# Gates of two token blocks by seven quarter products instead of eight, in a fused retention and feed-forward kernel

## The chip, the core and the metric

The kernel runs on one core of a Trainium2 chip. Its engines work side by side, each on its own queue of instructions: PE multiplies matrices (PEld is its loading of weights, which overlaps), DVE, ACT and POOL do elementwise work, and SP issues transfers. PE puts its results in PSUM, which the kernel's pools divide into eight banks of 128 x 512 float32 (`tr` 1, `qk` 2, `pv` 1, `st` 1, `ffn` 3); the other engines read them from there. The metric is the time of one execution in microseconds on the device, the median of the runs.

## The reference

Retention for 8 sequences of 8 heads, and a gated feed-forward layer on its result:

```python
scores = scale * np.matmul(q, k.transpose(0, 1, 3, 2))       # q, k, v: 8 x 8 x 576 x 64
Dmat = np.where(rel >= 0, gamma[:, None, None] ** rel[None, :, :], 0.0)
attn = np.matmul(scores * Dmat[None, :, :, :], v)
x = attn.transpose(0, 2, 1, 3).reshape(4608, 512)
gate = 1.0 / (1.0 + np.exp(-(x @ w_gate)))                   # w_gate, w_val: 512 x 1536
val = x @ w_val
out = gate * val @ w_out                                     # w_out: 1536 x 512
```

## The kernel before, in words

Both halves are interleaved: while PE does the feed-forward products of one block of tokens, the retention of the tokens of the next one is put between them. The tokens come in blocks: 0 to 511 first (written out by hand), then two of 256 tokens at 512 and 768 (`BLOCKS`), then blocks of 512 from 1024 on. The retention makes x transposed in bfloat16 (`xT`, model dimension on the partitions), in pairs of steps: `row` (q times k), `pt` (times the decay, on DVE), `new` (the step's share of the running state), `s` (the state's sum, on DVE), `sb` (the state cast to bfloat16, on ACT) and `val` (the result, cast into `xT` by ACT). Before that, POOL and DVE scale q and k by the decay (`qk`), POOL casts v, and SP's transposing transfers (or PE's `turn`, copied out as `T`) turn them.

The 1536 columns of the feed-forward layer are 12 chunks of 128 (`fc`), four to a unit u. In a block of 512 tokens, a unit's gates, a product of 512 x 512 by 512 x 512, are formed from quarters by seven products (`quarter_units`): product 1 is x's first quarter by the weights' first quarter, 2 the second quarters, 3 the fourth x quarter with a sum of weights, 4 a sum of x quarters (`xsum`) with the fourth weight quarter, and 5, 6 and 7 sums of weights by sums of x. In code: product 1 goes to bank `a` (`gatea`) and ACT copies it to bank `g` (`gateg`), on which product 2 adds; product 6 adds to `a`, and ACT keeps a copy `u2`; product 5 goes to bank `e` (`gatee`), and ACT keeps a copy `s5`; product 3 adds to `e`, and DVE adds `e` to `u2`; product 7 adds to `a`, and DVE adds `a` to `s5`; product 4 adds to `a`. Each of the four results gets its sigmoid on ACT. A product is four matmuls, of 128 x 128 weights by the quarter's columns. The weight sums (`wgt_sb` for gates, `wvt` for values, `wt_sb` for the output weights) are made once by DVE or POOL, before the block that first needs them.

In the two blocks of 256 tokens, gates and values are formed by full products (`h_units`): 12 groups of eight matmuls of 256 columns for each block, a gate pair `h_g` and its value pair `h_v` by turns, a sigmoid on ACT for each gate pair, a multiply on DVE for each value pair. Then come two output products (`op_units`) of 12 matmuls of 512 columns, which ACT copies to `ob` to be stored.

The order on every engine is the order in which the code is written (`manual_schedule`). In the blocks of 256, `ffn_units` yields after each group, and behind the i-th group of block w the loop at the end of the kernel puts what the table `SUMS_AT` lists for "w.i": weight sums (g, w, o, with their number and engine, v for DVE and p for POOL), the scaling and casting of later steps (c), a turn (t), the first batch's state (f); `PAIRS_AT` says behind which groups a pair of retention steps begins. `OP_CUTS` and `FIRST_OP_CUTS` say how many matmuls of 512 columns of the output products are cut into two of 256.

Of the kernel before, what the change touches and what calls it, by code (L numbers as in the profile page):

```python
# [9 lines left out]
FP32 = mybir.dt.float32  # L10
# [6 lines left out]
def kernel(  # L17
# [858 lines left out]
    def h_units(gvs, fcs, t0, n):  # L876

        for fc in fcs[::2]:
            gv_tile(gvs, t0, fc)
            both = made[t0, fc // 4][:, fc % 4:fc % 4 + 2, 0:n]  # L880
            for what, w_sb in (("g", wg_sb), ("v", wv_sb)):
                ps = ffn_psum.tile([P, 2, n], FP32, tag="ffn", name=f"h_{what}_{t0}_{fc}")
                for i in range(2):
                    for kc in range(NKC):
                        nc.tensor.matmul(ps[:, i], lhsT=w_sb[:, kc, (fc + i) * P:(fc + i + 1) * P],  # L885
                                         rhs=xT(kc, slice(t0, t0 + n)), start=(kc == 0), stop=(kc == NKC - 1))
                if what == "g":
                    nc.scalar.activation(out=both, in_=ps, func=AF.Sigmoid)
                else:
                    nc.vector.tensor_tensor(out=both, in0=both, in1=ps, op=ALU.mult)  # L890
                yield 8 * n
# [79 lines left out]
    first_w = {}  # L971

    def first_sums_begin(kind):

        u = NU - 1
        t = [osb.tile([P, 2, 2, 2 * P], BF16, tag="osb", name=f"first_{kind}_{i}") for i in range(1 if kind == "g" else 2)]
        first_w[kind] = ([wt3_sb["g"][i][u] for i in range(3)] if kind == "g" else
                         [t[0][:, 0], t[0][:, 1], t[1][:, 1]]) + [t[-1][:, 0]]

    def first_w_sum(kind, i, eng):  # L980

        a11, a12, a21, a22 = w_quarters(kind, NU - 1)
        s1, s2, s4, s3 = first_w[kind]
        to, a, b, op = ((s1, a21, a22, ALU.add), (s2, s1, a11, ALU.subtract), (s3, a11, a21, ALU.subtract),
                        (s4, a12, s2, ALU.subtract))[i]
        eng.tensor_tensor(out=to, in0=a, in1=b, op=op)

    def first_x_sum(i, eng):

        if 0 not in turned_x:  # L990
            turned_x[0] = [ld_pool.tile([P, 2, 2, 256], BF16, tag="xsum", name=f"xsum_0_{i}", bufs=SLOTS["xsum"])
                           for i in range(2)]
        t1, t2, t3, t4 = (turned_x[0][i][:, j] for i in range(2) for j in range(2))
        b11, b12, b21, b22 = (xT(slice(r, r + 2), slice(c, c + 256)) for r in (0, 2) for c in (0, 256))
# [7 lines left out]
    def quarter_units(gvs, t0):  # L1002

        BANKS = {("g", 0): [(tr_psum, "tr"), (pv_psum, "pv"), (qk_psum, "qk")],
# [4 lines left out]
                 ("w", 2): [(qk_psum, "qk"), (qk_psum, "qk"), (tr_psum, "tr")]}  # L1009
        waiting = []  # L1010
# [5 lines left out]
        def bank(kind, u, i):  # L1016
            pool, tag = BANKS[kind, u][i]
            more = {"written": True} if pool is ffn_psum and i == 1 else {}
            name = ("gate" if kind == "g" else "w") + "age"[i]
            return pool.tile([P, 2, 256], FP32, tag=tag, name=f"{name}_{t0}_{u}", **more)  # L1020

        def keep(kind, u, name, ps, eng=on_act):
            t = sum_tile([P, 2, 256], FP32, f"{kind}{name}_{t0}_{u}")
# [3 lines left out]
        def right(i):  # L1027
            x = xT(ALL, slice(t0, t0 + 512))
            t = turned_x[t0] if i > 3 else None
# [661 lines left out]
```

## Time and profile before

| | us |
|---|---|
| median of 3 runs | 303.05 (302.89 to 303.10) |
| the profiled execution | 303.61 |
| its span | 302.0 |
| PE busy in the span | 295.4 |
| first group of block 512 starts | 51.52 |
| first output product of block 512 starts | 63.20 |
| first group of block 768 starts | 69.78 |
| first output product of block 768 starts | 81.70 |
| block 1024 starts | 88.62 |

The span runs from the first to the last record of the execution, so 1.6 us of it lie around it. Times of rows are counted from the span's start. A row of a timeline gives start, duration (of the whole run of like instructions, "x8"), engine, line of the kernel, operation, output and inputs with the program's names, and in brackets the idle time before it with what ended it. In a row of grouped instructions the busy time and the mean duration in ns stand behind the bar. Matmul durations overlap, and their distance is read from the starts.

### The profile page before, as it was taken

To read this page: it belongs to the slowest core of one execution; us is meant where nothing else is said; L and a number is where in the kernel's file an instruction comes from. 1 tells how busy PE (TensorE), PEld (TensorE's weight loads), DVE (VectorE), ACT (ScalarE), POOL (GpSimd) and SP (SyncE) were. 2 spreads that over 40 slices of the span, in tenths; PEclk is the share of its full clock that TensorE was granted. 3 is DMA by queue.
4 is the path that set the end of the run, shared out by engine and by line. 5 is a ranking of instruction groups with operands and counts; after the bars stand their busy time and mean duration, and the time that the engine had idled before them with its cause. 6 is when DMAs were issued, how large, how long until landed. Compare 5 with 4: busy or idle time off the path is not lost.

```text
span 302.0 us, 10689 instructions
## 1 busy us (share of the span) xinstructions
PE 295.4 (98%) x4430; PEld 250.4 (83%) x4437; DVE 230.1 (76%) x439; ACT 204.6 (68%) x414; POOL 224.9 (74%) x253
## 2 busy tenths in 40 slices
PE   8999999999999999999999999999999999999994
PEld 3687876978868888888888888888888888888883
DVE  5967995686886998789748974896489848935793
ACT  6764574345369747985798589857985698559830
POOL 5775754846479898978997898789978947860780
PEclk9999999999999999999999999999999999999999
DMA  7999999979899979897759967976793165004013
GB/s 205 309 339 398 362 345 239 209 155 210 174 197 222 248 176 225 186 221 211 143 114 200 250 143 155 194 207 146 128 204 127 37 111 205 4 2 139 3 36 104
DMA packets 146464, 54.99 MB, mean 182 GB/s; under 512 B 124400, under 2 KB 139760, under 8 KB 146416
## 3 DMA queue, kind: packets, MB, share of 16 engines
q1 hardware_dynamic: 145328, 53.59, 73.3%
q10 hardware_dynamic: 1088, 0.72, 0.8%
q8 instruction: 34, 0.56, 0.8%
q14 instruction: 14, 0.11, 0.1%
HBM read 37.75 MB, written 9.44 MB: 156 GB/s over the span
## 4 chain that ended last, share of the span: by engine, by line
PE 86%; DMA 7%; SPq 4%; POOL 1%; issue 0%; ACT 0%; DVE 0%
PE gatea L1045 12%; PE wa L1045 12%; PE qa L1172 11%; PE qe L1172 9%; PE gatee L1045 6%; PE we L1045 6%; PE h_v L885 4%; PE h_g L885 3%; PE op L1305 3%; DMA wv<-in_moe_w_val_dram 3%; PE op L1548 3%; PE gateg L1045 3%; PE wg L1045 3%; SPq L186 3%; DMA wg<-in_moe_w_gate_dram 2%; PE val L717 2%
## 5 line engine op out<-in xcount | busy, mean ns | idle before, releaser
L1045 PEld LDWEIGHTS <-wg_sb 128*128 128x128 bf16 x348 | 34.0, 98 | 4.2
L1072 POOL TENSOR_TENSOR gv<-gv,wu 128x512 bf16<-128x512 bf16 x20 | 23.5, 1174 | 16.1 <-DVE wu L1084 16.0
L1172 PEld LDWEIGHTS <-gsum 128*128 128x128 bf16 x312 | 29.9, 98 | 3.7
L1045 PEld LDWEIGHTS <-wv_sb 128*128 128x128 bf16 x296 | 29.0, 98 | 3.4
L429 POOL TENSOR_TENSOR qk<-q,qtab 128x512 bf16<-128x512 f32 x28 | 30.1, 1073 | 1.4 <-DMA q<-in_q_dram 1.4
L1084 DVE TENSOR_TENSOR gu<-gatee,gu 128x512 f32<-128x512 f32 x22 | 15.2, 690 | 19.4 <-ACT gateg L1076 10.2
L1045 PEld LDWEIGHTS <-wgt_sb 128*128 128x128 bf16 x264 | 25.8, 98 | 3.0
L942 POOL TENSOR_TENSOR gsum<-gsum,gv 128x256 bf16<-128x256 bf16 (+1 forms) x20 | 17.6, 891 | 14.4 <-DVE gsum L942 12.6
L1045 PE MATMUL gatea<-xsum,wg_sb 128*128 128x256 bf16 x172 | 25.6, 273 | 0.0
L1172 PEld LDWEIGHTS <-gv 128*128 128x128 bf16 x228 | 21.8, 98 | 2.7
L429 POOL TENSOR_TENSOR qk<-k,ktab 128x512 bf16<-128x512 f32 x11 | 12.1, 1097 | 13.9 <-DMA k<-in_k_dram 9.6
L1087 DVE TENSOR_TENSOR gs<-gatea,gs 128x512 f32<-128x512 f32 x22 | 15.1, 688 | 9.4 <-PE gatea L1045 9.3
L942 POOL TENSOR_TENSOR gsum<-gv,gsum 128x256 bf16<-128x256 bf16 (+1 forms) x24 | 21.9, 921 | 0.2
L703 DVE TENSOR_TENSOR pt<-row,tri 128x512 bf16<-128x512 f32 x30 | 19.2, 681 | 2.9 <-PE row L686 2.7
L442 POOL TENSOR_TENSOR v<-v,ktab 128x512 bf16<-128x512 f32 x19 | 20.9, 1100 | 0.0
L1045 PE MATMUL wa<-xsum,wv_sb 128*128 128x256 bf16 x136 | 20.4, 273 | 0.0
L658 ACT CAST sb<-s 128x512 bf16<-128x512 f32 (+1 forms) x26 | 14.3, 569 | 8.4 <-DVE s L828 8.3
L787 ACT CAST xT<-val 128x512 bf16<-128x512 f32 x26 | 14.7, 592 | 7.0 <-PE val L733 7.0
L942 DVE TENSOR_TENSOR gsum<-gv 128x512 bf16<-128x512 bf16 (+1 forms) x34 | 18.7, 576 | 0.0
L1045 PEld LDWEIGHTS <-wvt 128*128 128x128 bf16 x168 | 16.4, 98 | 1.9
L942 POOL TENSOR_TENSOR gsum<-gv 128x256 bf16<-128x256 bf16 (+1 forms) x20 | 17.6, 880 | 0.0
L1070 ACT ACTIVATE gv<-gu 128x512 bf16<-128x512 f32 x22 | 14.0, 638 | 5.2 <-DVE gu L1084 5.2
(210 smaller groups left out, 882.6 us busy)
## 6 DMA issues: line engine op xcount, KB each, us to landing
k<-in_k_dram SPq DMA_DIRECT2D x26, 256.0 KB, 3.8
q<-in_q_dram SPq DMA_DIRECT2D x26, 256.0 KB, 4.2
v<-in_v_dram SPq DMA_DIRECT2D x26, 256.0 KB, 4.6
out_dram<-ob SPq DMA_DIRECT2D x24, 256.0 KB, 2.8
wg<-in_moe_w_gate_dram SPq DMA_DIRECT2D x12, 256.0 KB, 5.3
wv<-in_moe_w_val_dram SPq DMA_DIRECT2D x12, 256.0 KB, 5.2
wo<-in_moe_w_out_dram SPq DMA_DIRECT2D x12, 256.0 KB, 5.3
v32p<-in_v_dram SPq DMA_DIRECT2D x6, 256.0 KB, 4.7
```

What stands on the lines that cost most here:

```text
L429: eng.tensor_tensor(out=to, in0=by_halves(loaded[s][1 - i]), in1=tab, op=ALU.mult)
L442: nc.gpsimd.tensor_tensor(out=natural["v", s], in0=loaded[s][2], in1=tab, op=ALU.mult)
L658: eng(out=both_steps["sb", b, c][:, js], in_=both_steps["s32", b, c][:, js])
L703: nc.vector.tensor_tensor(out=t[:, y, 0:n].rearrange("p i m t -> p (i m) t"), in0=rows_tile[ss[0]][y][:, 0:n].rearrange("p i m t -> p (i m ...
L787: nc.scalar.copy(out=to, in_=src)
L885: nc.tensor.matmul(ps[:, i], lhsT=w_sb[:, kc, (fc + i) * P:(fc + i + 1) * P], rhs=xT(kc, slice(t0, t0 + n)), start=(kc == 0), stop=(kc == ...
L942: eng.tensor_tensor(out=to, in0=a, in1=b, op=op)
L1045: nc.tensor.matmul(ps[:, f], lhsT=w[:, kc, f * P:(f + 1) * P], rhs=x[:, kc], start=(first and f == 0 and kc == 0), stop=(f == 1 and kc == ...
L1072: eng.tensor_tensor(out=to, in0=to, in1=src[:, part], op=ALU.mult)
L1084: nc.vector.tensor_tensor(out=me["u2"], in0=e, in1=me["u2"], op=ALU.add)
L1087: nc.vector.tensor_tensor(out=me["s5"], in0=a, in1=me["s5"], op=ALU.add)
L1172: nc.tensor.matmul(ps[:, b], lhsT=left(fp)[:, b * P:(b + 1) * P], rhs=right(fp), start=(first and fp == 0 and b == 0), stop=(fp == NFC // ...
```

## The change

In the two blocks of 256 tokens the gates are now made by the seven quarter products too, of 128 columns each: `quarter_units` takes the number of tokens, and a half of it, m, is the width of a quarter. The values stay full products. The strings `SHORT` give the order in a block: g and two digits is a gate product (the first digit is the place of the unit in `UNITS`, the second the number of the product), v a pair of value chunks, V a single one, m the multiply by DVE of the oldest value product whose turn has not come. The units come in the order 1, 2, 0, in the output products too. The blocks' token sums are made by `block_x_sum`, of which block 512 has three on DVE and one on POOL, and block 768 four on DVE. The weight sums of the gates are all made in the first block, and those of the values later; copies move from DVE to ACT; and the cuts and groups are placed anew. In block 1024 the gate products 4, 6 and 7 are made in two halves of columns.

```diff
-        for i, ((pool, tag), eng) in enumerate(zip(VALS, (on_act, on_dve))):
+        for i, ((pool, tag), eng) in enumerate(zip([(ffn_psum, "ffn")] * 2 if s == 1 else VALS, (on_act, on_act if s == 1 else on_dve))):
...
-                (nc.vector.tensor_copy if hh == y else nc.sync.dma_start)(
+                (nc.scalar.copy if hh == y else nc.sync.dma_start)(
...
-    def h_units(gvs, fcs, t0, n):
-
-        for fc in fcs[::2]:
-            gv_tile(gvs, t0, fc)
-            both = made[t0, fc // 4][:, fc % 4:fc % 4 + 2, 0:n]
-            for what, w_sb in (("g", wg_sb), ("v", wv_sb)):
-                ps = ffn_psum.tile([P, 2, n], FP32, tag="ffn", name=f"h_{what}_{t0}_{fc}")
...
+    SHORT = (("g05 g01 g11 v0 g02 g06", "g12 g03 g16 g15", "g07 v2 g04 m g13 g21", "g17 v6 m g26", "g14", "g25 v4", "m", "m", "g22 g23", "g27 v8 g24 V11 m m V10 m", ""),
+             ("g11 g01 v0 g05", "g06 g15", "g02 g16 g12 g07 g03 g21 g04", "g17 v4 m g25 g13 g14", "m v6", "g26 g23 m", "g22 v8 g27 v2 m", "g24 m", "V10 V11 m", "m", ""))
+    UNITS = (1, 2, 0)
+
+    def h_units(gvs, t0, n):
+
+        quarter, _ = quarter_units(gvs, t0, n)
+        mults = []
+        for steps in SHORT[t0 > BLOCKS[0][0]]:
+            cols = 0
+            for x in steps.split():
+                if x == "m":
+                    quarter.settle()
+                    to, by = mults.pop(0)
+                    nc.vector.tensor_tensor(out=to, in0=to, in1=by, op=ALU.mult)
+                    continue
+                u = UNITS[int(x[1]) if x[0] == "g" else int(x[1:]) // 4]
+                if x[0] == "g":
+                    cols += quarter("g", u, int(x[2]))
+                    continue
...
+    def block_x_sum(t0, n, i, eng):
...
+        to, a, b = ((t1, b12, b11), (t3, b22, b12), (t2, b22, t1), (t4, b21, t2))[i]
         eng.tensor_tensor(out=to, in0=a, in1=b, op=ALU.subtract)
...
+        if n < 512:
+            BANKS["g", 0][2] = (st_psum, "st")
+            BANKS["g", 1][2] = (ffn_psum, "ffn")
...
-            for f in range(2):
-                for kc in range(2):
-                    nc.tensor.matmul(ps[:, f], lhsT=w[:, kc, f * P:(f + 1) * P], rhs=x[:, kc],
...
+            parts = 2 if t0 == BLOCKS[2][0] and kind == "g" and i in (4, 6, 7) else 1
+            for f, kc, part in ((f, kc, part) for f in range(2) for kc in range(2) for part in range(parts)):
+                cols = slice(part * m // parts, (part + 1) * m // parts)
+                nc.tensor.matmul(ps[:, f, cols], lhsT=w[:, kc, f * P:(f + 1) * P], rhs=x[:, kc, cols],
...
-    OP_CUTS = (6, 11, 0, 0)
+    OP_CUTS = (0, 0, 0, 11)
...
-    for i in (0, 1, 3):
-        w_sums("w", i, 0, nc.vector)
-    for i in (0, 1, 3):
-        w_sums("g", i, 1, nc.vector)
-
-    FIRST_OP_CUTS = 20
+    for u in (1, 0):
+        for i in (0, 1, 3, 2):
+            w_sums("g", i, u, nc.vector)
+
+    FIRST_OP_CUTS = 44
...
+    X_SHORT = ('vvvp', 'vvvv')
+    for i in range(3):
+        block_x_sum(512, 256, i, nc.vector if X_SHORT[0][i] == "v" else nc.gpsimd)
...
-    store(opps[2], 2 * P, on_dve)
+    store(opps[2], 2 * P, on_act)
...
-    SUMS_AT = ("0.0:c03p 0.1:f00p 0.3:g00p 0.3:w10v 0.3:w11v 0.6:t01p 0.7:o10p 0.8:c02v "
...
+    SUMS_AT = ("0.1:c03p 0.2:f00p 0.3:w00p 0.4:w01p 0.5:o10v 0.6:w03p 0.7:t01p 0.7:c02v 0.9:c05p 0.12:w10v "
...
-    PAIRS_AT = ((0, 10), (0, 11), (1, 10), (1, 0))
+    PAIRS_AT = ((0, 9), (0, 13), (1, 9), (1, 5))
...
+        if w == 1:
+            for i in range(4):
+                block_x_sum(t0, n, i, nc.vector if X_SHORT[1][i] == "v" else nc.gpsimd)
```

Three places of the order. On ACT, around the start of block 768, before the change: `ob_640` is the copy of the last output product of block 512, `sb` a state's cast.

```order
L658 CAST sb_2_0_1644<-s32_2_0_1632 128x512
L917 COPY ob_640_1657<-op_512_1_1622 128x512
L658 CAST sb_2_1_1659<-s32_2_1_1646 128x512
L888 ACTIVATE gv_768_0_1661<-h_g_768_0_1662 128x2x256
L888 ACTIVATE gv_768_0_1661<-h_g_768_2_1683 128x2x256
L888 ACTIVATE gv_768_1_1705<-h_g_768_4_1706 128x2x256
```

And in the changed kernel:

```order
L658 CAST sb_2_0_1712<-s32_2_0_1703 128x512
L932 COPY ob_640_1721<-op_512_1_1696 128x512
L658 CAST sb_2_1_1741<-s32_2_1_1714 128x512
L1078 COPY gateg_768_2_1755<-gatea_768_2_1750 128x256
L1078 COPY gateg_768_1_1763<-gatea_768_1_1758 128x256
L1028 COPY gs5_768_1_1779<-gatee_768_1_1774 128x256
L1028 COPY gu2_768_1_1785<-gatea_768_1_1758 128x256
L1028 COPY gs5_768_2_1792<-gatee_768_2_1787 128x256
L1072 ACTIVATE gv_768_1_1757<-gateg_768_1_1763 128x2x128
```

Behind the same three operations, one sigmoid for a group of the block is replaced by copies of product 1, 5 and 6 of two units, before the first sigmoid.

On DVE, from the second `pt` of the pair before block 768 on, before the change:

```order
L703 TENSOR_TENSOR pt_2_1619<-row_2_1_1536,tri_274 128x512
L830 COPY s32_2_0_1632<-new_2_0_1569 128x256
L828 TENSOR_TENSOR s32_2_0_1632<-s32_2_0_1632,new_2_1_1570 128x256
L828 TENSOR_TENSOR s32_2_1_1646<-s32_2_0_1632,new_2_0_1569 128x256
L828 TENSOR_TENSOR s32_2_1_1646<-s32_2_1_1646,new_2_1_1570 128x256
L324 TENSOR_TENSOR wt_sb_278<-wo_sb_277 128x512
L890 TENSOR_TENSOR gv_768_0_1661<-gv_768_0_1661,h_v_768_0_1673 128x2x256
```

And in the changed kernel:

```order
L703 TENSOR_TENSOR pt_2_1693<-row_2_1_1610,tri_274 128x512
L830 COPY s32_2_0_1703<-new_2_0_1643 128x256
L828 TENSOR_TENSOR s32_2_0_1703<-s32_2_0_1703,new_2_1_1644 128x256
L324 TENSOR_TENSOR wt_sb_278<-wo_sb_277,wt_sb_278 128x512
L828 TENSOR_TENSOR s32_2_1_1714<-s32_2_0_1703,new_2_0_1643 128x256
L828 TENSOR_TENSOR s32_2_1_1714<-s32_2_1_1714,new_2_1_1644 128x256
L995 TENSOR_TENSOR xsum_768_0_1743<-xT_768_1701 128x2x128
L995 TENSOR_TENSOR xsum_768_1_1744<-xT_768_1701 128x2x128
L995 TENSOR_TENSOR xsum_768_0_1743<-xT_768_1701,xsum_768_0_1743 128x2x128
L995 TENSOR_TENSOR xsum_768_1_1744<-xT_768_1701,xsum_768_0_1743 128x2x128
L1089 TENSOR_TENSOR gs5_768_1_1779<-gatea_768_1_1758,gs5_768_1_1779 128x256
```

A sum of output weights stands between the state's sums now, and the block's four token sums behind them, ahead of the first addition of a gate product.

On POOL, between the cast of v for step 3 and the scaling of step 5's k and q, before the change:

```order
L444 CAST v_3_1193<-v32_3_1157 128x512
L365 TENSOR_TENSOR wgt_sb_279<-wg_sb_275 128x512
L324 TENSOR_TENSOR wt_sb_278<-wo_sb_277 128x512
L429 TENSOR_TENSOR qk_4_1401<-k32_4_1182,ktab1_249 128x2x4x64
L429 TENSOR_TENSOR qk_4_1401<-q32_4_1184,qtab1_248 128x2x4x64
L444 CAST v_4_1406<-v32_4_1186 128x512
L429 TENSOR_TENSOR qk_5_1423<-k32_5_1408,ktab1_249 128x2x4x64
```

And in the changed kernel:

```order
L444 CAST v_3_1280<-v32_3_1188 128x512
L365 TENSOR_TENSOR wvt_0_873<-wv_sb_276 128x512
L365 TENSOR_TENSOR wvt_1_874<-wvt_0_873,wv_sb_276 128x512
L365 TENSOR_TENSOR wvt_2_875<-wv_sb_276,wvt_1_874 128x512
L429 TENSOR_TENSOR qk_4_1428<-k32_4_1269,ktab1_249 128x2x4x64
L429 TENSOR_TENSOR qk_4_1428<-q32_4_1271,qtab1_248 128x2x4x64
L444 CAST v_4_1433<-v32_4_1273 128x512
L429 TENSOR_TENSOR qk_5_1450<-k32_5_1435,ktab1_249 128x2x4x64
```

Three sums of value weights stand ahead of step 4's scaling, where one of gate weights and one of output weights stood.

More of the change, by code (lines that the diff above doesn't have):

```diff
@@ new lines @@
+    UNITS = (1, 2, 0)
[14 more added lines that the diff above has]
+                    continue
+                fc = 4 * u + int(x[1:]) % 4
+                many = 2 if x[0] == "v" else 1
+                both = made[t0, u][:, fc % 4:fc % 4 + many, 0:n]
+                ps = ffn_psum.tile([P, many, n], FP32, tag="ffn", name=f"h_v_{t0}_{fc}")
+                for i in range(many):
@@ L884, in h_units @@
                     for kc in range(NKC):
-                        nc.tensor.matmul(ps[:, i], lhsT=w_sb[:, kc, (fc + i) * P:(fc + i + 1) * P],
+                        nc.tensor.matmul(ps[:, i], lhsT=wv_sb[:, kc, (fc + i) * P:(fc + i + 1) * P],
                                          rhs=xT(kc, slice(t0, t0 + n)), start=(kc == 0), stop=(kc == NKC - 1))
[L887 to L890, printed above, removed]
@@ L969, in x_sums @@
             (nc.gpsimd if by == "p" else nc.vector).tensor_tensor(out=to, in0=a, in1=b, op=ALU.subtract)
[L971 to L994, printed above, removed]
+    def block_x_sum(t0, n, i, eng):
+        if t0 not in turned_x:
+            turned_x[t0] = [ld_pool.tile([P, 2, 2, 256], BF16, tag="xsum", name=f"xsum_{t0}_{j}", bufs=SLOTS["xsum"])
+                            for j in range(2)]
+        m = n // 2
+        t1, t2, t3, t4 = (turned_x[t0][j][:, y, :, 0:m] for j in range(2) for y in range(2))
+        b11, b12, b21, b22 = (xT(slice(r, r + 2), slice(t0 + c, t0 + c + m)) for r in (0, 2) for c in (0, m))
         to, a, b = ((t1, b12, b11), (t3, b22, b12), (t2, b22, t1), (t4, b21, t2))[i]
@@ L1657 @@
         assert w != 1 or paired == len(PAIRS_AT)
+        assert not [x for x in sums_at if x[0] == w]
         while len(pending) > (w == 1):
```

76 lines of the change are left out of this document (40 added, 36 removed), and 3 rows, old and new, of the table SUMS_AT.

## The prediction

> **What bounds the kernel now.** I read the page first (busy shares, granted clock, chain that ended last), then the waits of PE, then the timelines of the four compute engines from 38 us to 80 us, where the change lies.
>
> ```profile
> PE 295.4 (98%) x4430; PEld 250.4 (83%) x4437; DVE 230.1 (76%) x439; ACT 204.6 (68%) x414; POOL 224.9 (74%) x253
> PEclk9999999999999999999999999999999999999999
> PE 86%; DMA 7%; SPq 4%; POOL 1%; issue 0%; ACT 0%; DVE 0%
> ```
>
> ```profile
> PE idle L242 <- DVE blank L229: 1.1, 1, 1.1
> ...
> PE op L1548 <- issue: 0.2, 1, 0.2
> ```
>
> PE is busy for 98% of the span at an undisturbed clock, and carries 86% of the chain; the rest of the chain is the loading at the start. PE's list of waits has five rows, of which the first and the last stand here; none is of L885 or L1305, the lines of the two blocks of 256 tokens. So a PE instruction taken out there shortens the end by its own time, and every new wait of PE lengthens it by the whole wait.
>
> The price of a matmul is the distance between starts, since the durations overlap. PE's timeline:
>
> ```profile
> 46.24 0.64 PE L563 MATMUL pvp<-ptp,vp 64*64 64x128 bf16 x32
> ...
> 50.21 0.61 PE L630 MATMUL turn<-ident,qk 128*128 128x128 bf16 x8
> 50.66 1.03 PE L1548 MATMUL op<-wo_sb,gv 128*128 128x512 bf16 x4
> 51.52 1.04 PE L885 MATMUL h_g<-xT,wg_sb 128*128 128x256 bf16 x8
> ...
> 57.64 0.61 PE L630 MATMUL turn<-ident,qk 128*128 128x128 bf16 x8
> 58.08 1.04 PE L885 MATMUL h_v<-xT,wv_sb 128*128 128x256 bf16 x8
> ...
> 61.67 0.45 PE L686 MATMUL row<-T 64*64 64x64 bf16 x32
> ...
> 63.20 2.77 PE L1305 MATMUL op<-wo_sb,gv 128*128 128x512 bf16 x17
> ...
> 69.78 1.04 PE L885 MATMUL h_g<-xT,wg_sb 128*128 128x256 bf16 x8
> 70.67 1.03 PE L885 MATMUL h_v<-xT,wv_sb 128*128 128x256 bf16 x8
> ```
>
> Four matmuls of 512 columns take 51.52 - 50.66 = 0.86 us, 0.215 each. Seven groups of eight with 256 columns lie between 51.52 and 57.64: 6.12/56 = 0.109 each. Eight of 128 columns, each with its own weight load, take 50.66 - 50.21 = 0.45 us, 0.056 each.
>
> **The sum on PE.** Each block loses 48 gate matmuls of 256 columns (48 x 0.109 = 5.23 us) and gains 84 of 128 columns (84 x 0.056 = 4.70): -0.53, for two blocks -1.06. In block 1024, 36 gate matmuls become 72 of half the columns: 36 x (2 x 0.056 - 0.109) = +0.11. Cuts of output matmuls: 24 more and 6 fewer, 18 x (2 x 0.109 - 0.215) = +0.05. Together **-0.90 us**, if PE waits nowhere.
>
> The 56 ns stand on runs of eight; the change has runs of up to 28. The loads give the upper bound:
>
> ```profile
> L885 PEld LDWEIGHTS <-wg_sb 128*128 128x128 bf16 x96 | 9.4, 98 | 1.3
> ```
>
> Were a product paced by a load of 98 ns, a block would take 84 x 0.098 = 8.23, +3.0 us for each. I take 56, because those eight turns have just such loads before each matmul. [...]
>
> **What the edits cost off PE.** ACT had six sigmoids of 512 columns in each block and gets 21 operations of 256 columns (three copies and four sigmoids for each of three units), and two more copies that DVE had. DVE gets six additions, and in block 768 four token sums.
>
> ```profile
> 51.50:61.60 10.10, 10.10 (x97) 8.97 (x95) 6.57 (x13) 4.05 (x7) 8.70 (x9) 1.00 1.00 222
> ...
> 69.80:79.40 9.60, 9.60 (x90) 8.48 (x87) 6.61 (x12) 3.99 (x7) 4.18 (x5) 1.00 0.87 192
> ```
>
> ```profile
> 289.99 0.65 ACT L1254 COPY s<-qa 128x256 f32<-128x256 f32 x2 [1.04 <-PE qa L1248]
> ```
>
> ```profile
> L1444 ACT ACTIVATE gv<-hg 128x256 bf16<-128x256 f32 x4 | 1.4, 384 | 1.4 <-PE hg L1438 1.4
> ```
>
> ```profile
> L828 DVE TENSOR_TENSOR s<-s,new 128x256 f32<-128x256 f32 x39 | 16.2, 416 | 0.9
> ```
>
> In the windows the engines' columns stand as PE, PEld, DVE, ACT, POOL. Two copies of 256 columns end after 0.65 us, so one of 0.38 is followed by the next after about 0.28. 21 such operations take 5.9 to 8.0 us instead of about 3: ACT has 7 to 9 of 10 us to do. DVE goes from 6.6 to about 9.1 (six times 0.416). Neither becomes the bound by its sum; single operations come late. The places, with the price that I take and its ends:
>
> (1) *Block 768, first value product (v0).* It uses the bank of the last output product of block 512, which ACT's copy `ob` must empty.
>
> ```profile
> 70.03 0.58 ACT L917 COPY ob<-op 128x512 f32<-128x512 f32 x1 [0.40 <-PE op L1305]
> 70.52 0.62 ACT L658 CAST sb<-s 128x512 bf16<-128x512 f32 x1
> 71.04 0.60 ACT L888 ACTIVATE gv<-h_g 128x512 bf16<-128x512 f32 x1
> ```
>
> The copy starts 0.25 us after the output product ends (69.78 to 70.03), and ACT is free again 0.49 later: the bank is free 0.74 to 0.83 us after that end. Now the first value product comes 0.89 us after it (70.67), covered by a full gate product; then only g11 and g01 are ahead of it, 8 x 0.056 = 0.45. PE waits 0.3 to 0.4: **0.35**. Product g06 needs the copy of g01, which stands behind `ob` and the state's cast: 0.25 + 0.49 + 0.52 + 0.28 + 0.38 = 1.92 us after the block's start, against PE's own 1.89; the wait before it covers that.
>
> (2) *Block 768, g04.* It overwrites what DVE's addition of g07 reads. PE's result reaches the next engine after 0.25, the addition takes 0.42, and only g03 and g21 (0.45) lie between: **0.2** (0 to 0.3). In block 512 a value product of 0.87 lies there.
>
> (3) *Block 512, turn 1.* Its second half takes the bank of h_v_10, whose multiply needs the last sigmoid of unit 2. g14 ends 6.2 us after the block's start; 0.25 + 0.38 + a multiply of 0.69 make 7.5, and PE is there at 7.5. A weight sum stands ahead on DVE:
>
> ```profile
> 61.58 0.87 DVE L324 TENSOR_TENSOR wt_sb<-wo_sb 128x512 bf16<-128x512 bf16 x1
> ...
> 69.83 1.17 DVE L324 TENSOR_TENSOR wt_sb<-wo_sb 128x512 bf16<-128x512 bf16 x1
> ```
>
> ```profile
> 60.02 1.15 POOL L324 TENSOR_TENSOR wt_sb<-wo_sb 128x512 bf16<-128x512 bf16 x1
> 61.13 1.04 POOL L429 TENSOR_TENSOR qk<-k,ktab 128x512 bf16<-128x512 f32 x1
> ...
> 68.67 1.04 POOL L429 TENSOR_TENSOR qk<-k,ktab 128x512 bf16<-128x512 f32 x1 [4.77 <-DMA k<-in_k_dram]
> 69.68 1.04 POOL L429 TENSOR_TENSOR qk<-q,qtab 128x512 bf16<-128x512 f32 x1
> ```
>
> Both sums of DVE end 0.28 us after the POOL product that runs beside them (61.13 + 1.04, then 62.45; 69.68 + 1.04, then 71.00). So a DVE sum of two SBUF operands waits for POOL, and can make this one later by 0.4: **0.1** (0 to 0.4). [...]
>
> (4) *First block, pair 2.* DVE does eight sums of gate weights ahead of the four `ptp` products, where six weight sums stood.
>
> ```profile
> 38.91 0.47 DVE L365 TENSOR_TENSOR wvt<-wv_sb 128x512 bf16<-128x512 bf16 x1
> ...
> 42.78 2.47 DVE L492 TENSOR_TENSOR ptp<-qkp,trip 128x512 bf16<-128x512 f32 x4
> ```
>
> Six took 3.87 us, 0.65 each; two more take 0.8 to 1.3, so the last `ptp` ends at 46.1 to 46.5 instead of 45.25. PE's pvp starts at 46.24 and wants it about 0.1 later: **0.1** (0 to 0.2).
>
> (5) *The rest, nothing.* Rows and new states of block 512 now come behind all products of the block, so that the 0.89 us of h_v between 62.31 and 63.20 no longer lie behind them; the state's casts then stand 0 to 0.1 late at the next val, and the end of the range holds that. The three token sums on DVE and one on POOL for block 512 lie in DVE's idle time before the turn's copy and in POOL's wait for loads.
>
> ```profile
> 50.86 0.42 DVE L632 COPY T<-turn 128x512 bf16<-128x512 bf16 x1 [0.92 <-PE turn L630]
> ...
> 50.75 0.61 POOL L444 CAST v<-v 128x512 bf16<-128x512 f32 x1 [1.06 <-DMA v<-in_v_dram]
> ```
>
> POOL does three sums ahead of qk_4 where it did two, so qk_4 comes 1.15 us later, with SP's transpose that waits for it and the k, q, v loads queued behind that:
>
> ```profile
> 63.38 1.80 SPq L448 DMA_TRANSPOSE T<-qk  x1
> 65.28 0.53 SPq L171 DMA_DIRECT2D k<-in_k_dram  x1
> ```
>
> The k load lands 68.67 - 65.28 = 3.4 us after its issue, so POOL's qk_5 moves to about 69.8. Its own readers come several us later; what it meets there is the first rival below.
>
> Waits: 0.35 + 0.2 + 0.1 + 0.1 = 0.75 (ends 0.3 and 1.4). Net -0.90 + 0.75 = **-0.15 us**. The profiled execution took 303.61 (span 302.0, and 1.6 around it) and would take 303.4; it stands 0.56 above the median of the runs, 303.05, which becomes 302.9.
>
> **The rivals.** *Token sums of block 768 meet POOL (slower).* DVE's third token sum is needed by g06, about 71.2. After pt_2 DVE's way to the sums is 69.83 - 66.86 = 2.97 us in these rows, plus a weight sum of 0.33 that is now between:
>
> ```profile
> 66.86 1.29 DVE L703 TENSOR_TENSOR pt<-row,tri 128x512 bf16<-128x512 f32 x2 [0.37 <-PE row L686]
> ```
>
> pt_2 starts about 0.4 earlier, so the sums start near 69.75, and qk_5 near 69.8. If POOL begins before the second sum, that sum ends at 69.8 + 1.04 + 0.28 = 71.1, and the third stands behind POOL's second product, to 72.2: g06 waits 1.0 us, net +0.85, **303.9**. If two sums are through first, nothing happens. The two starts are too close to tell; it decides at a shift of 0.2 us.
>
> *No waits worth naming (faster).* If copies are visible to PE earlier than the rows' durations say, and DVE and POOL don't meet, only part of (1) remains: **302.3**. For it speaks that ACT and DVE have some us of room in the sum; against it, that v0's and g04's waits need no coincidence.
>
> *The short products run at the pace of their loads.* At 98 ns the gates of the two blocks cost 6.0 us more instead of 1.06 less: 303.05 + 6.0 + 0.16 for the halves and cuts = **309**, all further waits hidden in it. The eight turns at 56 ns speak against it. [...]
>
> **How the numbers follow.** No change can be told within 0.2% of 303.05, 0.6 us. Forecast, most of the gain given back (302.5 to 303.5): 0.43, nearly all within 0.2%. No waits (302.0 to 302.4): 0.29. Token sums behind POOL (303.7 to 304.2): 0.21. Pace of loads: 0.03. Several of the small waits at their upper ends (above 303.6): 0.04. So faster 0.30, within 0.2% 0.42, slower 0.28. The range from 302.1 to 304.2 leaves out the last two cases and the edges of the second and third. The forecast's own range is 302.5 to 303.5.
>
> **What would show it.** Right: the 84 short matmuls of a block start every 56 ns; PE's waits list h_v <- ACT ob of about 0.35 and a gate product <- DVE of about 0.2 in block 768, a turn <- DVE and pvp <- DVE below 0.2. Wrong: a wait of a gate product for DVE xsum near 71 us (first rival); no new rows in PE's waits and a span near 301.1 (second); starts every 80 to 100 ns (third). A wait in a place that I did not name, above all one that comes from loads that SP issues later, would also make it wrong.

## The result, and the profile after

The changed kernel takes 305.9 us (median of six runs, 304.76 to 306.32) against 303.13 for the kernel before (six runs, 302.89 to 303.50): a ratio of 1.0082, 95% interval 1.0060 to 1.0103. It is slower by about 2.8 us, outside the range given. The six times lie in two groups, two at 304.8 and four near 306; the profiled execution shown here is one of 304.78, its span 303.1. The medians and ratios below leave out one execution, that of 312.84 us in e2_old_cuts, which counts as slow, being over 1.5% above the fastest of its kernel.

The page of the changed kernel, its busy shares, clock, chain and the queue that carries instructions:

```profile
PE 295.2 (97%) x4563; PEld 252.3 (83%) x4563; DVE 234.8 (77%) x455; ACT 213.1 (70%) x448; POOL 226.4 (75%) x254
...
PEclk9999999999999999999999999999999999999999
...
q8 instruction: 35, 0.57, 0.8%
...
PE 88%; DVE 3%; SPq 3%; DMA 2%; ACT 1%; issue 1%; POOL 0%; DVEq 0%; ACTq 0%
```

PE is busy for 0.2 us less, in a span that is 1.1 us longer. The busy time is too coarse to show the saving (294.9 and 295.4 us in two more traces of the kernel before, 295.4 and 295.0 of the changed one), since a record that outlasts its turn (0.22 us for a matmul of 128 columns, 0.056 from start to start) covers about the first 0.16 us of each wait. Waits of PE in the changed kernel, as line, what it waited for, us, times, longest:

```profile
PE qkp L485 <- ACT qT L476: 0.6, 2, 0.4
PE op L1308 <- issue: 0.6, 1, 0.6
PE turn L630 <- DVE gv L890: 0.3, 1, 0.3
PE h_v L902 <- ACT ob L932: 0.3, 1, 0.3
```

Before, none of these lines waited except qkp. PE's timeline at the places:

```profile
51.25 0.39 PE L1047 MATMUL gatee<-xsum,wgt_sb 128*128 128x128 bf16 x4
51.47 0.61 PE L1047 MATMUL gatea<-xT,wg_sb 128*128 128x128 bf16 x8
51.92 1.04 PE L902 MATMUL h_v<-xT,wv_sb 128*128 128x256 bf16 x8
...
58.69 0.39 PE L630 MATMUL turn<-ident,qk 128*128 128x128 bf16 x4
59.38 0.38 PE L630 MATMUL turn<-ident,qk 128*128 128x128 bf16 x4 [0.31 <-DVE gv L890]
...
69.52 0.61 PE L1047 MATMUL gatea<-xT,wg_sb 128*128 128x128 bf16 x8
70.42 1.03 PE L902 MATMUL h_v<-xT,wv_sb 128*128 128x256 bf16 x8 [0.28 <-ACT ob L932]
...
73.07 0.39 PE L1047 MATMUL gatea<-xT,wg_sb 128*128 128x128 bf16 x4
73.60 0.61 PE L1047 MATMUL gatea<-xsum,wg_sb 128*128 128x128 bf16 x8
...
86.12 2.25 PE L1308 MATMUL op<-wo_sb,gv 128*128 128x512 bf16 x18
88.95 0.71 PE L1308 MATMUL op<-wo_sb,gv 128*128 128x256 bf16 x5 [0.59 <-issue]
```

Twelve matmuls of 128 columns start in 51.92 - 51.25 = 0.67 us: 0.056 each, as priced. The lost time of a wait is best taken between starts, since a matmul's record outlasts its turn: the two halves of the turn lie 0.69 us apart instead of 0.22 (0.47 lost), the first value product of block 768 starts 0.90 after eight short matmuls instead of 0.45 (0.44 lost with the decimals), g04 0.53 after its predecessor instead of 0.22 (0.30). And the last output product of block 768 stands still inside one run of matmuls that wait for no data: "issue", 0.75 us lost between starts.

Three traces of each kernel, by the start of a stage's first matmul (taken from the traces' records; the third of the kernel after and the second and third of before are from the runs a2_after, b1_before and b2_before below, the second of after from e1_again):

| stage, us | before, three traces | after, three traces |
|---|---|---|
| start to first output product | 37.63, 37.74, 37.18 | 37.08, 37.50, 37.49 |
| to block 512 | 13.90, 13.82, 13.82 | 14.17, 14.20, 14.26 |
| block 512 to its output product | 11.67, 11.67, 11.69 | 11.73, 11.73, 11.73 |
| to block 768 | 6.58, 6.58, 6.90 | 6.55, 6.55, 6.55 |
| block 768 to its output product | 11.92, 11.84, 11.84 | 12.04, 12.13, 13.07 |
| to block 1024 | 6.92, 6.93, 6.93 | 7.93, 8.72, 8.33 |
| block 1024 to its first output product | 18.77, 18.77, 18.99 | 18.95, 18.95, 18.95 |
| first output product of the first block to the last matmul | 260.05, 259.70, 260.26 | 261.42, 262.33, 262.96 |
| behind the last matmul | 4.29, 4.27, 4.27 | 4.57, 4.66, 4.56 |

Each of the two blocks should have lost 0.53 us and took 0.05 and 0.2 to 1.2 more. The largest part, 1.0 to 1.8 us, lies where no gate is computed: between the output products of block 768 and block 1024.

### The profile page after: what moved, and what is told of

It is laid out like the page before. It is cut to its first block, busy times and chain, and to the rows that moved or that the text cites. A ratio compares the mean times of both kernels' runs of the same rounds, so it can differ in the third digit from the quotient of the medians.

```text
span 303.1 us, 11006 instructions
## 1 busy us (share of the span) xinstructions
PE 295.2 (97%) x4563; PEld 252.3 (83%) x4563; DVE 234.8 (77%) x455; ACT 213.1 (70%) x448; POOL 226.4 (75%) x254
## 4 chain that ended last, share of the span: by engine, by line
PE 88%; DVE 3%; SPq 3%; DMA 2%; ACT 1%; issue 1%; POOL 0%; DVEq 0%; ACTq 0%
PE gatea L1047 14%; PE wa L1047 12%; PE qa L1175 11%; PE qe L1175 9%; PE gatee L1047 7%; PE we L1047 6%; PE gateg L1047 4%; PE op L1549 3%; PE h_v L902 3%; PE wg L1047 3%; PE op L1308 3%; SPq L186 3%; DMA wg<-in_moe_w_gate_dram 2%; PE val L717 2%; PE qa L1251 2%; PE hv L1376 2%
## 5 line engine op out<-in xcount | busy, mean ns | idle before, releaser
L1047 PEld LDWEIGHTS <-wg_sb 128*128 128x128 bf16 x472 | 41.5, 98 | 4.4 <-issue 0.3
L1086 DVE TENSOR_TENSOR gu<-gatee,gu 128x512 f32<-128x512 f32 (+1 forms) x28 | 17.7, 633 | 21.8 <-ACT gateg L1078 10.0
L1047 PEld LDWEIGHTS <-wgt_sb 128*128 128x128 bf16 x348 | 30.8, 98 | 3.3 <-issue 0.2
L1047 PE MATMUL gatea<-xsum,wg_sb 128*128 128x256 bf16 (+1 forms) x248 | 30.8, 252 | 0.1
L1089 DVE TENSOR_TENSOR gs<-gatea,gs 128x512 f32<-128x512 f32 (+1 forms) x28 | 17.7, 631 | 10.1 <-PE gatea L1047 10.0
L1072 ACT ACTIVATE gv<-gu 128x512 bf16<-128x512 f32 (+1 forms) x28 | 16.5, 590 | 6.5 <-DVE gu L1086 6.4
L1072 ACT ACTIVATE gv<-gs 128x512 bf16<-128x512 f32 (+1 forms) x28 | 16.4, 586 | 5.3 <-DVE gs L1089 5.2
L1072 ACT ACTIVATE gv<-gatea 128x512 bf16<-128x512 f32 (+1 forms) x28 | 15.7, 566 | 3.0 <-PE gatea L1047 2.8
```

Of the source, the lines that this page charges most:

```text
L1047: nc.tensor.matmul(ps[:, f, cols], lhsT=w[:, kc, f * P:(f + 1) * P], rhs=x[:, kc, cols], start=(first and f == 0 and kc == 0 and part == 0 ...
L1072: nc.scalar.activation(out=to, in_=src[:, part], func=AF.Sigmoid)
L1086: nc.vector.tensor_tensor(out=me["u2"], in0=e, in1=me["u2"], op=ALU.add)
L1089: nc.vector.tensor_tensor(out=me["s5"], in0=a, in1=me["s5"], op=ALU.add)
```

## The experiments

Two theories of the stretches without a shown wait. **A, the loading of instructions:** PE's program is loaded in pieces of 16 KB (35 transfers with 0.57 MB on q8 in the page above), and PE stands still where one comes late; 252 more PE instructions move the borders of the pieces to other places of the program. **B:** waits for data, of which the profile does not show the cause. The same kernel once more (e1_again):

> The changed kernel once more, for a second trace and more times. Six times of it lie in two groups (304.8 and about 306), and the trace at hand is one of 304.8, whose new waits in the two blocks sum to about the saved 1.06 us, and which besides has two stretches in which PE waits for nothing shown: 0.23 us inside val at 84.7 and 0.75 us inside the last output product at 88.1. Theory A (instruction loading: both stretches end 1.5 us after a 16 KB instruction transfer): a run near 306 shows the same waits for data and one or more further or longer unexplained stretches, 1.2 us in all, each ending about 1.5 us after such a transfer. Theory B (data waits vary): the 1.2 us lie in a longer wait for DVE or ACT, at the token sums near 71 us above all.

It measured 306.67 us (before, measured beside it, 303.33; ratio 1.0098, 1.0072 to 1.0124). Its waits:

```profile
PE op L1308 <- issue: 1.4, 1, 1.4
...
PE turn L630 <- DVE gv L890: 0.3, 1, 0.3
PE h_v L902 <- ACT ob L932: 0.3, 1, 0.3
```

The waits for data are those of the first trace to 0.01 us; what differs is the still stretch in the same output product, 1.57 us lost instead of 0.75. The run near 306 differs from that near 304.8 there (0.8) and in a later start (0.4). The numbers of the instructions tell more. Here is every stretch of more than 0.15 us after 80 us without a shown wait, in the eight traces that hold all matmuls (e5_moved_cuts has none), with the number of the instruction behind it in PE's order (a matmul counts two, its load of weights and itself) and the end of the last 16 KB transfer of the instruction queue:

| run | lost, us | at instruction | number modulo 256 | transfer ended | PE went on, later by |
|---|---|---|---|---|---|
| after | 0.22 | 2494 | 190 | 83.55 | 1.39 |
| after | 0.75 | 2750 | 190 | 87.44 | 1.51 |
| e1_again | 0.19 | 2494 | 190 | 84.15 | 1.30 |
| e1_again | 1.57 | 2750 | 190 | 88.89 | 1.39 |
| e2_old_cuts | 1.07 | 4286 | 190 | 141.40 | 1.43 |
| e2_old_cuts | 2.32 | 5310 | 190 | 174.30 | 1.39 |
| e2_old_cuts | 0.34 | 6334 | 190 | 209.61 | 1.32 |
| e2_old_cuts | 1.99 | 6590 | 190 | 213.78 | 1.43 |
| e3_no_op_cuts | 1.47 | 7358 | 190 | 231.94 | 1.30 |
| e4_before_44 | 0.41 | 3518 | 190 | 116.38 | 1.42 |
| e6_waits | 0.61 | 2750 | 190 | 89.72 | 1.30 |
| e7_cuts_ahead | 0.61 | 2494 | 190 | 82.71 | 1.44 |
| e7_cuts_ahead | 1.09 | 2750 | 190 | 87.57 | 1.41 |

All thirteen stand at a border of 256 instructions, in kernels with different work there, and end 1.3 to 1.5 us after a transfer. The count agrees: in the first trace of the changed kernel 35 transfers of 16 KB stand beside 9,126 PE instructions (4,563 matmuls and as many loads of weights), 261 to a transfer. Numbered in order, with 446 as the first border, every border has its transfer: in the eight traces PE passes no border after 30 us less than 1.29 us after the end of the transfer of the same number, and most of these transfers start only after PE has passed the border before (in the first trace of the changed kernel 25 of 32, by 0.01 to 2.34 us, and the other seven 0.06 to 1.56 us ahead of it). In the changed kernel PE passes border 2494 at 84.94, the transfer for the next piece starts at 86.56, ends at 87.44, and PE goes on at border 2750 at 88.95: 4.0 us from border to border, in the second trace 4.8 (85.45, 88.01, 88.89, 90.28). The instructions between 2494 and 2750 are 110 matmuls of 64 columns (1.2 us) and 18 of the cut output product (2.1): 3.3 us, so PE waits. Few microseconds of work in a piece do not alone make a stop: the piece from 7102 to 7358 takes 2.53 us in the first trace and passes, as its successor's transfer starts 0.01 us behind the border, not 1.6 to 2.6. What sets that delay is not shown.

**The cuts put back (e2_old_cuts)**, 108 PE instructions fewer, the same work:

```diff
-            parts = 2 if t0 == BLOCKS[2][0] and kind == "g" and i in (4, 6, 7) else 1
+            parts = 1
-    OP_CUTS = (0, 0, 0, 11)
+    OP_CUTS = (6, 11, 0, 0)
-    FIRST_OP_CUTS = 44
+    FIRST_OP_CUTS = 20
```

> The changed kernel with the cuts of the kernel before: 20 cut matmuls in the first block's output products, OP_CUTS (6, 11, 0, 0), no halves in block 1024: 54 matmuls (108 PE instructions) fewer than the changed kernel, the same work. Theory A: the stretches move to other places in the program, and the time changes by some tenths up to 1.5 us, either way. Theory B: only the matmuls' own cost goes, 36 x 3 ns + 18 x 3 ns = 0.16 us; the time stays within 0.3 us of the changed kernel's and keeps its two groups.

309.40 us (three executions, 307.78 to 311.43; ratio 1.0193, 1.0132 to 1.0254), 2.7 above the changed kernel measured beside it (306.67). That the time moves is A's, but by nearly twice the 1.5 us that I gave as the most:

```profile
PE qe L1175 <- issue: 2.3, 2, 2.1
PE qa L1175 <- issue: 1.8, 1, 1.8
...
PE val L733 <- issue: 0.9, 1, 0.9
```

With 54 matmuls fewer the stretches moved into a step of retention and output products of later blocks. The profiled execution is the one of 312.84, with 5.7 us in these four; so the trace shows where the stops lie, and not what they cost in the other three. It holds one thing more: 0.44 us after the longest stop the granted clock falls to 0.5 for 3.4 us (176.13 to 179.54), and 16 matmuls of 256 columns start 0.213 us apart instead of 0.109, 1.65 us more. The cuts of matmuls, which cost some 3 ns each (2 x 0.109 - 0.215 us), set what lies between the borders.

**Without the cuts of the last output product (e3_no_op_cuts):**

```diff
-    OP_CUTS = (0, 0, 0, 11)
+    OP_CUTS = (0, 0, 0, 0)
```

> The changed kernel with OP_CUTS (0, 0, 0, 0): eleven matmuls (22 PE instructions) fewer, all in the output product in which PE stood still for 0.75 us at 88.1. Theory A: instructions behind that place come 22 earlier; the still stretch moves by some matmuls or changes its length, also in later places. Theory B: no change beyond 0.03 us.

306.57 us (1.0095, 1.0069 to 1.0121): the time of the changed kernel, which B had. But the trace decides against B: block 1024 starts 7.17 us after the first output product of block 768, not 7.93 or 8.72, and 1.47 us are lost at instruction 7358 instead.

```profile
PE val L733 <- issue: 1.3, 1, 1.3
```

**The kernel before, with more cuts (e4_before_44):**

```diff
-    FIRST_OP_CUTS = 20
+    FIRST_OP_CUTS = 44
```

> The kernel before with 44 instead of 20 cut matmuls in the first block's output products: 48 PE instructions more, no other change. Theory A: the time moves by more than the 0.05 us of the cuts, up to 1 us, by new stretches without a wait shown. Theory B: 303.1, as before.

305.42 us (1.0061, 1.0041 to 1.0082): 24 cuts, worth 0.07 us of matmul time, cost 2.1 us, more than A's 1 us. Its trace holds one still stretch of 0.41 us, at a border, and a new wait for data:

```profile
PE kTp L466 <- POOL kp L412: 0.9, 1, 0.9
...
PE gatee L1045 <- DVE gs L1024: 0.5, 1, 0.5
...
PE val L733 <- issue: 0.2, 1, 0.2
```

From the first output product on it takes 1.20 us more than before's first trace, 0.4 at the border and 0.7 at gatee; and that execution came to the first output product 1.3 us later, through code that the edit does not touch. So this run shows that such stops come into the kernel before as well, not that they are all of its loss.

**The cuts moved behind the place (e5_moved_cuts):**

```diff
-    OP_CUTS = (0, 0, 0, 11)
+    OP_CUTS = (0, 0, 0, 0)
...
-            parts = 2 if t0 == BLOCKS[2][0] and kind == "g" and i in (4, 6, 7) else 1
+            parts = 2 if t0 == BLOCKS[2][0] and kind == "g" and i in (3, 4, 6, 7) else 1
```

> The changed kernel with the eleven cuts taken out of the last output product of block 768 (22 PE instructions fewer) and product 3 of block 1024 made in halves too (24 more), so that all later instructions stand nearly where they did. In the traces so far every unexplained stop of PE after 80 us ends at an instruction whose number leaves 190 by 256, 1.3 to 1.5 us after a 16 KB instruction transfer. Theory A (loading of pages of 256 instructions): instruction 2750 now lies behind the output product, some 1.4 us later, so the stop of 0.75 to 1.57 us in the output product is gone; the stop at 2494 (0.2 us) stays; later blocks stay without stops. 304.0 to 305.0, about 1.2 us below the changed kernel. Theory B (the stop belongs to the output product or to what DVE and POOL do there): it stays, 305 to 306.5.

305.67 us (before, measured beside it, 303.65; 1.0058, 1.0033 to 1.0084). Both stops are gone, also the 0.2 us at 2494 that A had kept, and none came in their place later:

```profile
86.20 0.32 PE L733 MATMUL val<-T,sb 64*64 64x64 bf16 x16 [0.15 <-DVE glance L754]
86.45 2.76 PE L1308 MATMUL op<-wo_sb,gv 128*128 128x512 bf16 x12
89.06 1.04 PE L1047 MATMUL gatea<-xT,wg_sb 128*128 128x256 bf16 x8
...
91.30 0.62 PE L1047 MATMUL gatea<-xsum,wgt_sb 128*128 128x128 bf16 x8 [0.33 <-DVE xsum L984]
```

The twelve matmuls of the output product run through, and block 1024 starts 7.17 us after the first one. But two waits for DVE that the stops had covered come to light: 0.32 us lost at a `val` (for DVE's `glance`), which is why 7.17 is still more than the 6.93 of before, and 0.49 at a gate product (for a token sum). The place was A's, the time of 304.0 to 305.0 was missed by 0.7; the interval overlaps that of the changed kernel (1.0060 to 1.0103), so it is the trace that shows the finding, not the time.

**The cuts one product ahead (e7_cuts_ahead):**

```diff
-    OP_CUTS = (0, 0, 0, 11)
+    OP_CUTS = (0, 0, 11, 0)
```

> The changed kernel with its eleven cuts in the first output product of block 768 instead of the second: the same matmuls, the same number of instructions. Theory A: the two steps of retention between them stand 22 instructions later, so instructions 2494 to 2750 hold the end of the first product and nearly all of the 64-column matmuls, about 2.5 us of work instead of 3.3: the stop moves to instruction 2750 at the start of the second product and is about 0.8 us longer, 1.5 to 2.4 us; 306 to 307.5. Theory B: as the changed kernel, 304.8 to 306.7, with the stop where it was or in the cut product.

306.44 us (1.0113, 1.0078 to 1.0148), which lies in the ranges of both theories; the trace tells them apart.

```profile
83.15 0.55 PE L630 MATMUL turn<-ident,qk 128*128 128x128 bf16 x7
84.15 0.22 PE L630 MATMUL turn<-ident,qk 128*128 128x128 bf16 x1 [0.45 <-issue]
...
86.36 1.68 PE L1308 MATMUL op<-wo_sb,gv 128*128 128x512 bf16 x7
88.98 1.24 PE L1308 MATMUL op<-wo_sb,gv 128*128 128x512 bf16 x5 [0.93 <-issue]
```

Now PE also stops before the last of eight turns, which is where instruction 2494 lies in this order, and in the uncut product at 2750. B has no reason for a stop in the middle of a turn. That the stop at 2750 would be longer than before was not borne out (1.09 against 0.75 and 1.57): the instructions between the two borders take 3.7 us there, not the 2.5 that I gave, and 4.8 us pass from border to border, as in the changed kernel's second trace.

**The waits for data (e6_waits)**, on top of e5:

```diff
-    "0.7:t01p", "0.15:o01v"
+    "0.8:t01p", "1.3:o01v"
-    "g17 v6 m g26", "g14", "g25 v4"
+    "g17 v6 m g14", "g26", "g25 v4"
-    "g11 g01 v0 g05", "g06 g15", "g02 g16 g12 g07 g03 g21 g04", "g17 v4 m g25 g13 g14"
+    "g11 g01 g05 v0", "g06 g15", "g02 g16 g12 g07 g03 g21 g17", "g04 v4 m g25 g13 g14"
```

> The kernel of the moved cuts with the named waits for data taken away by other places: turn 1 one group later; g14 ahead of g26 in block 512; in block 768 g05 ahead of the first value product, g17 ahead of g04, and the weight sum o01 behind the token sums instead of ahead of them. If the waits cost what the traces show (0.47 at the turn, 0.15 at g26, 0.44 at h_v, 0.30 at g04: 1.36 us), about 1.0 of them goes, the first value product keeping about 0.2: 1.0 us below the moved cuts, 303.0 to 304.0. If later waits take their place (DVE or ACT late by as much), less than 0.5 goes.

304.19 us (1.0024, 1.0000 to 1.0049), 1.5 below e5 where 1.0 was expected, and 0.2 above the range given; its ten times reach from 303.35 to 305.63, and the profiled execution is the slowest. Block 512 went from 11.73 to 11.35 us. Block 768 took 13.37 in that execution:

```profile
72.03 0.40 PE L1047 MATMUL gatea<-xsum,wgt_sb 128*128 128x128 bf16 x4 [0.67 <-DVE xsum L995]
...
75.80 0.38 PE L1047 MATMUL gatee<-xsum,wgt_sb 128*128 128x128 bf16 x4 [0.41 <-ACT gv L1072]
```

```profile
69.60 1.33 DVE L995 TENSOR_TENSOR xsum<-xT 128x256 bf16<-128x256 bf16 x2
70.85 1.74 DVE L995 TENSOR_TENSOR xsum<-xT,xsum 128x256 bf16<-128x256 bf16 x2
```

```profile
69.71 1.07 POOL L429 TENSOR_TENSOR qk<-k,ktab 128x512 bf16<-128x512 f32 x1 [4.73 <-PE op L1308]
70.74 1.08 POOL L429 TENSOR_TENSOR qk<-q,qtab 128x512 bf16<-128x512 f32 x1
```

That is the prediction's first rival as it was written: the second token sum ends 0.15 us after POOL's first product (70.93 and 70.78), the third stands behind POOL's second, and the gate product that needs it starts 0.83 us late. A stop came back too, 0.61 us at border 2750, now in block 1024's first gate product, where e5 had none: its transfer started 2.82 us after PE had passed the border before.

**POOL's sum moved (e8_waits_pool)**, on top of e5: turn 1, g14, g05 and o01 as in e6, g04 left, w03 on POOL from 0.6 to 1.4 and o23 on DVE from 1.15 to 2.2.

```diff
-    "0.6:w03p", "1.15:o23v"
+    "1.4:w03p", "2.2:o23v"
```

> The kernel of the moved cuts, with turn 1 one group later, g14 ahead of g26, g05 ahead of the first value product of block 768, and three weight sums elsewhere: o01 (DVE) and w03 (POOL) behind the start of block 768, o23 (DVE) behind the token sums of block 1024. g04 stays where it was. In the last kernel with waits taken away the token sums of block 768 met POOL's scaling of step 5 (PE waited 0.83 us for DVE xsum), because that scaling came near 69.7; with one POOL sum fewer ahead of it, it should come 1.1 us earlier and be over before the third token sum is needed. If the waits are independent, block 512 takes 11.3 us from its first product to its first output product, block 768 11.7, and block 1024 starts without the 0.5 us wait for DVE xsum: 1.0 to 1.3 us below the moved cuts, 0 to 0.5 us below or at the kernel before in the same call. If the token sums still meet POOL, block 768 takes 12.4 or more and it ends 0.5 us or more above the kernel before.

304.56 us (before, measured beside it, 303.85; 1.0020, 0.9996 to 1.0044): 1.15 below e5 by the ratios, as expected, and the kernel before to within the interval, not the gain of up to 0.5 us over it. Its trace has block 512 in 11.32 and block 768 in 12.01 us, of which 0.14, 0.19 and 0.30 are waits at the first value product, at g06 and at g04, with 0.28 more at the `val` ahead of block 1024 and nothing lost in it; from the first output product to the last matmul 259.93 us, against 260.0 before.

**g25 later (e9_g25_later)**, on top of e8:

```diff
-    "g02 g16 g12 g07 g03 g21 g04", "g17 v4 m g25 g13 g14"
+    "g02 g16 g12 g07 g03 g21 g17", "g04 v4 m g13 g14 g25"
```

> The last kernel (moved cuts, waits taken away, POOL sum moved) with g17 ahead of g04 in block 768 as well, and g25 behind g13 and g14. g04's wait for DVE (0.30 us) should go, since one more product (0.22) lies ahead of it, and g25's bank should be free in time, since two more products lie ahead of it: block 768 takes 11.75 us instead of 12.0, all else as it was; 0 to 0.6 us below the kernel before in the same call. If ACT's order only puts the wait elsewhere, block 768 stays at 12.0 and the time at the last kernel's, 0.5 us above the kernel before.

304.96 us (before 303.99; 1.0036, 1.0014 to 1.0059). g04's wait went, but block 768 still took 11.94, and block 1024 took 19.57 us to its first output product instead of 18.98. No gain.

**Both kernels again, on one chip (b1_before, a2_after, b2_before):**

> The kernel before once more, for a second trace of it. So far its stages stand on one trace. Theory A: PE's waits in the two blocks are none again, no stop of more than 0.3 us at an instruction whose number leaves 190 by 256 after 45 us, and from the first output product of the first block to the last matmul it takes 260.0 us again (within 0.3), while the time up to that product varies by up to 1 us from run to run. If the kernel before shows stops of the changed kernel's size as well, the comparison of stages stands on chance.

> The changed kernel a third time, on the same chip. Theory A: the waits for data are again 0.47 (turn), 0.44 (first value product of block 768), 0.30 (g04) and 0.15 (g26) to within 0.03, the stop at instruction 2750 between 0.6 and 1.7 us, and from the first output product to the last matmul it takes 261.4 to 262.4 us, 1.4 to 2.4 above the kernel before. The end behind the last matmul takes 4.5 to 4.7 us against 4.3.

> As the first of these three, a third trace of the kernel before: 260.0 us (within 0.3) from the first output product of the first block to the last matmul, 4.2 to 4.4 behind it.

303.36, 306.73 and 303.35 us. The table of stages holds them: before repeats to 0.3 us from the first output product on, with no stop of that size; after takes 1.2 to 3.3 more. a2_after ends 0.6 beyond what I gave, since its token sums met POOL as well. Of its two "issue" waits the one of 1.2 is the stop in the last output product of block 768 again (1.37 lost); at the other a matmul's record is missing:

```profile
PE op L1308 <- issue: 1.4, 2, 1.2
...
PE gatea L1047 <- DVE xsum L995: 0.6, 1, 0.6
```

```profile
70.36 1.33 DVE L995 TENSOR_TENSOR xsum<-xT 128x256 bf16<-128x256 bf16 x2
71.62 1.74 DVE L995 TENSOR_TENSOR xsum<-xT,xsum 128x256 bf16<-128x256 bf16 x2
```

```profile
70.40 1.14 POOL L429 TENSOR_TENSOR qk<-k,ktab 128x512 bf16<-128x512 f32 x1 [5.54 <-DMA k<-in_k_dram]
71.51 1.08 POOL L429 TENSOR_TENSOR qk<-q,qtab 128x512 bf16<-128x512 f32 x1
```

The start of PE's gate products was held for 0.79 us, in the changed kernel itself.

## Why the prediction was wrong

*The saving on PE* was right: 56 ns for a short matmul also in runs of twelve, and block 512, which e9 leaves with 0.16 us of waits, takes 11.27 us there against 11.68 before: 0.57 less but for that wait, where 0.53 was forecast. The pace of the loads, 98 ns each (third rival), is excluded.

*The waits that were named* came, and were under-sized: first value product 0.35 forecast, 0.44 measured; g04 0.2, 0.30; the turn 0.1, 0.47; pvp 0.1, nothing; and g26, not named, 0.15. Together 0.75 forecast and 1.37 measured, which alone turns -0.15 into +0.47 us. The turn shows how: DVE's weight sum ahead of the multiply was in time, and it was ACT that was late.

```profile
57.26 0.70 DVE L324 TENSOR_TENSOR wt_sb<-wo_sb 128x512 bf16<-128x512 bf16 x1
58.64 1.28 DVE L890 TENSOR_TENSOR gv<-gv,h_v 128x512 bf16<-128x512 bf16 x2 [0.69 <-ACT gv L1072]
```

```profile
57.65 0.42 ACT L1072 ACTIVATE gv<-gs 128x256 bf16<-128x256 f32 x1
57.97 0.35 ACT L1028 COPY gu<-gatea 128x256 f32<-128x256 f32 x1
58.22 0.39 ACT L1072 ACTIVATE gv<-gatea 128x256 bf16<-128x256 f32 x1
```

I let the last sigmoid begin 0.25 us after g14; two operations stand ahead of it on ACT in the order, 0.57 us. ACT had room in the sum and none at that place.

*The first rival* (token sums behind POOL) came in one of three traces of the changed kernel, with 0.79 us against the 1.0 priced. It hangs on when k of step 5 lands: POOL's qk starts at 68.12 and 68.40 us in the two traces without it, and at 70.40 in the one with it, where 69.8 was forecast.

*What failed is the step "the rest, nothing"*: the sum had no term for the instructions themselves. I counted what the 36 halves and 18 cuts cost in matmul time, 0.16 us, and not that 252 more PE instructions shift the borders of the pieces in which PE's program is loaded. They fall so that 256 instructions between two borders hold most of a step of retention and 18 matmuls of the cut output product, and PE stops there for 0.75 to 1.6 us, and for 0.2 at the border ahead. The page of before showed the queue (34 instruction transfers on q8). The 0.2 us of "issue" in its list of waits are no such stop: each of the three traces of before has 4,430 matmuls for 4,437 loads of weights, and one of the missing records is there (loads at 47.18 and 47.19, the next matmul at 47.41). e5 takes both stops away, e7 and e2 make others.

The whole by the means of three traces: between the first output product and the last matmul 2.2 us more, of which -0.90 is the work, +1.37 the four waits, about +1.4 the two stops, +0.26 the token sums, and +0.36 the stage ahead of block 512. That is 2.5; the rest is two stages that took 0.24 longer before (6.69 against 6.55 us to block 768, 190.16 against 190.06 from block 1024's first output product on).

The stage ahead of block 512 is another meeting of DVE and POOL that the sum had at nothing. PE's transpose of q waits for DVE's second `qp`, 0.38 to 0.47 us lost in the three traces of the changed kernel. In the first of them, and in e3, which has the same instructions there:

```profile
35.75 0.96 DVE L412 TENSOR_TENSOR qp<-q32p,qtab 128x512 bf16<-128x512 f32 x1
35.55 0.61 POOL L314 CAST wo_sb<-wo 128x512 bf16<-128x512 f32 x1 [0.27 <-DMA wo<-in_moe_w_out_dram]
```

```profile
36.44 0.68 DVE L412 TENSOR_TENSOR qp<-q32p,qtab 128x512 bf16<-128x512 f32 x1
35.71 0.61 POOL L314 CAST wo_sb<-wo 128x512 bf16<-128x512 f32 x1 [0.29 <-DMA wo<-in_moe_w_out_dram]
```

In these three and in e6 the first `qp` begins 0.05 to 0.2 us after such a cast and takes 0.95 to 1.11 us; in the three traces of before and in e3, e5, e7, e8 and e9 it takes 0.68 or 0.69, and this wait is missing. The cast begins when a load of output weights lands; what sets that is not shown.

Behind the last matmul it is 0.3 us more in all kernels made from the changed one and in none made from before; the last output lands later there, and why is open.

No kernel here was measured faster than the one before. Whether the two blocks can keep the saved microsecond is open: with the stops and most waits removed (e8) the traces are equal and the times within the interval.

## What to carry to other kernels

On an engine that is always busy, count the instructions of a change and not their time alone: here PE stood still thirteen times at a border of 256 instructions, for 0.19 to 2.32 us, in the changed kernel (0.75 and 1.57 us) behind a piece with 110 short matmuls and 18 of an output product, and an edit of 22 instructions (e3) was enough to take one from instruction 2750 to 7358. In the traces such a stop has no releaser ("issue") and stands at the same remainder of the instruction's number (190 by 256); a matmul whose record is missing looks alike (0.2 us of "issue" before, with 4,430 matmuls for 4,437 loads of weights), so the loads have to be counted against the matmuls. And an engine with room in the sum can still be late at a single hand-over, as ACT, busy for 70% of the span, was at the turn (0.47 us lost): go through its order operation by operation at every place where PE takes a bank.

## What was not expected of the hardware

At the thirteen stops a piece of 256 PE instructions took 2.9 to 5.1 us from the border before to its first use: 0.6 to 2.8 until the transfer starts, 0.9 to 1.7 for it, 1.3 to 1.5 until PE goes on. The longest stop was 2.3 us (e2), and the clock at 0.5 behind it is the only such place ahead of the last matmul in the fourteen traces; whether the stop caused it is not shown, and behind the stop of 1.99 us in the same trace the clock stayed. Twenty-four cut matmuls, 0.07 us of work, made the kernel before 2.1 us slower, only part of it at a border.
